# Chunks 2 to 6 of the first MLP product as seven half-size products, with one staging area for q and k and another order of work

## The chip, the cores and the metric

The kernel runs on one core of a Trainium2 chip. The metric is the device time of one execution in microseconds (us), and lower is better. The five engines of a core are named here as in the profile: PE (TensorE) multiplies, PEld is its loading of weights, DVE is VectorE, ACT is ScalarE, POOL is GpSimd, and SP issues transfers.

## What is computed

Causal attention with 16 beacon keys in front of 576 tokens, for 8 batches of 8 heads with 64 columns each, and then a two-layer MLP with a squared relu over all 4608 tokens:

```python
k_all = np.concatenate([beacon_k, k], axis=2)          # q, k, v: (8, 8, 576, 64), beacons: (8, 8, 16, 64)
v_all = np.concatenate([beacon_v, v], axis=2)
scores = scale * np.matmul(q, k_all.transpose(0, 1, 3, 2))
scores = np.where(causal, -1000000000.0, scores)       # beacons are seen by all
a = np.exp(scores - scores.max(-1, keepdims=True))
a /= a.sum(-1, keepdims=True) + 1e-09
x = np.matmul(a, v_all).transpose(0, 2, 1, 3).reshape(4608, 512)
h = x @ w_in                                           # 512 x 2048
out = (np.maximum(h, 0.0) ** 2) @ w_out                # 2048 x 512
```

## The kernel before

All work is cut into small operations with names (`add(...)` in the code). Each has the engines it may run on, what it needs, which buffers it takes from a pool and gives back, and a function that emits its instructions. A list written out in the code, `SEQUENCE`, says in which order they are emitted; `@A`, `@D` or `@P` behind a name picks ACT, DVE or POOL. Every engine then works through its own instructions strictly in that order. Nothing is decided at run time.

**Attention.** Batches 0 and 1 come in by strided transfers (`sld`, `fld`) and are transposed on PE. From batch 2 on, `ld` loads rows of q, k and v to a staging pool `stg` in fp32, `cast` writes them as bf16 to `qb`, `kb` (two areas each, used in turn) or `vb`, all on POOL, and `tr` transposes q and k by a transfer to `qT`, `kT`. Four pairs of heads make a batch. `qk` (line 631) computes transposed scores into PSUM, `exp` (L729, L653) writes exponentials to `pt` on ACT, `mask` (L750) takes the minimum with a triangle `tri` on DVE for the diagonal tiles, `av` (L771) multiplies by v with a column of ones, and `norm` (L788, L790) divides into `xn`. `xtp` with `xte` on PE, or `xt` by transfers, put the result, transposed, into the ring `xT` of 1728 tokens.

**MLP.** Nine chunks of 512 tokens. The first product of chunk j (`s1.j...`) writes to `g[j % 2]` after a relu (`relu`) and a square (`sq`); the second product (`s2.j...`) reads it, and `ev` moves its result to `osb`, which `st` stores.

- Plain form of the first product (chunks 0 to 6, L1073): 16 blocks of four matmuls of 512 columns, each block in one PSUM bank, one relu per block, one square per two blocks. Chunk 0 is done in two parts of tokens. Where the ring wraps (chunks 3 and 6) each matmul is two.
- Form with seven products (`add_first_both`, chunks 7 and 8, L950): the weights are split in four quarters, and the tokens in even and odd ones. Seven products of half size (16 matmuls of 256 columns each) replace eight. Differences of weights (`asum`, L897, kept in the q/k area when attention no longer needs it) and of inputs (`xsum`, L930) are made first. Before it, `pull` copies the ring's tokens, even and odd apart, to a dense area on POOL.
- The second product is plain in chunks 0 and 1 (L1123) and in the seven-product form from chunk 2 on (L1182); `sum` (L1154) makes its sums of `g`, in an area `sum_area` for three of them.

In the seven-product form a chain "x" uses the same PSUM bank for products 1, 6, 7 and 4: each adds to what stands there, and after each the running sum is copied out (in the first product by `hold`, named `c1`, `u2`, `u3`, and `c21` for the last; in the second by `ev`). So the next product of the chain waits for the copy. Products 5 and 3 share a chain "y" in the same way, and product 2 has a bank "z". A `plus` on DVE adds a y or z result to a held copy and writes `g`; relu and square follow as separate instructions.

PSUM has two `strip` buffers of two banks and four `ps` banks. In chunks 7 and 8 the x chain of the first product uses strips; before them the strips belong to the scores.

## Time and profile before

| | us |
|---|---|
| median of 3 runs | 329.97 (329.48 to 330.12) |
| span of the profiled execution | 327.7 |
| PE busy | 315.9 |
| DVE busy | 231.9 |
| ACT busy | 225.7 |
| POOL busy | 101.1 |

The span goes from the first to the last instruction of one profiled execution. Its own time with what lies around the instructions is not listed; the runs are 1.8 to 2.4 us longer than this span, the median 2.3. In the profile a row of a group gives the line, the engine and operation, what it writes and reads, how often it ran, its busy time, the mean time of one in ns, and the idle time before it with what ended that. A row of a timeline gives the start and the length in us first. Busy times of an engine count overlapping instructions once.

### The profile page before, as it was taken

The numbers are of one execution on the slowest core, as the hardware profiler recorded it, in microseconds if no ns is written. First come the engines' busy times: TensorE is split into PE (matmuls) and PEld (weight loads), VectorE is DVE, ScalarE is ACT, GpSimd is POOL, SyncE is SP. The second block draws the span as 40 slices with busy tenths as digits, with TensorE's granted clock in tenths as the row PEclk, the third lists the DMA queues.
The fourth block names the chain that finished last, engine by engine and source line by source line (L and its number), as shares of the span: only waits on it lengthen the run. The fifth ranks groups of instructions, "written<-read, shape, count | busy, mean of one in ns | idle before, by whom it ended". The sixth has DMA issues, their size and how long they took to land.

```text
span 327.7 us, 8732 instructions
## 1 busy us (share of the span) xinstructions
PE 315.9 (96%) x3582; PEld 227.6 (69%) x3582; DVE 231.9 (71%) x487; ACT 225.7 (69%) x332; POOL 101.1 (31%) x149
## 2 busy tenths in 40 slices
PE   2999999999999999999999999999999999999995
PEld 1478785544565558888866565776788788888884
DVE  3777886534655899587864788768865797897871
ACT  4867796458874984777766889767837664695931
POOL 9854713404532450424033403641100252000000
PEclk9999999999999999999999999999999999999999
DMA  8999998899999999999999998997913210110033
GB/s 159 220 205 215 206 169 170 168 214 204 205 177 201 240 219 171 178 244 230 180 138 215 221 181 204 202 207 156 225 23 130 46 28 2 69 61 0 2 148 111
DMA packets 145602, 51.98 MB, mean 159 GB/s; under 512 B 132506, under 2 KB 140570, under 8 KB 145562
## 3 DMA queue, kind: packets, MB, share of 16 engines
q1 hardware_dynamic: 135901, 42.32, 65.7%
q0 software_dynamic: 8512, 8.49, 15.4%
q10 hardware_dynamic: 1149, 0.62, 0.9%
q8 instruction: 28, 0.46, 0.6%
q14 instruction: 12, 0.10, 0.1%
HBM read 37.22 MB, written 9.44 MB: 142 GB/s over the span
## 4 chain that ended last, share of the span: by engine, by line
PE 85%; DMA 8%; SPq 1%; ACT 1%; POOL 1%; DVE 1%; issue 1%; ACTq 0%; POOLq 0%; DVEq 0%
PE ps L1073 26%; PE ps L1182 21%; PE ps L771 9%; PE ps L1123 8%; PE strip L631 6%; PE strip L950 4%; PE ps L950 3%; DMA stg<-in_q_dram 3%; PE strip L1182 2%; DMA kT<-qk_area 2%; PE ps L631 2%; DMA osb<-in_q_dram 2%; DMA stg<-in_v_dram 2%; PE ps L839 1%; SPq L822 1%; PE ps L474 1%
## 5 line engine op out<-in xcount | busy, mean ns | idle before, releaser
L1073 PE MATMUL ps<-xT,w_in 128*128 128x512 bf16 (+6 forms) x640 | 106.3, 315 | 0.6 <-ACT pt L729 0.6
L1073 PEld LDWEIGHTS <-w_in 128*128 128x128 bf16 x640 | 56.2, 98 | 34.8 <-issue 1.6
L729 ACT ACTIVATE pt<-strip 128x1024 bf16<-128x1024 f32 (+3 forms) x77 | 69.6, 955 | 7.8 <-PE strip L631 7.7
L1088 ACT ACTIVATE g<-ps 128x512 bf16<-128x512 f32 (+2 forms) x82 | 44.4, 551 | 20.1 <-PE ps L1073 17.2
L342 POOL CAST qk_area<-stg 128x512 bf16<-128x512 f32 (+2 forms) x60 | 39.9, 672 | 53.7 <-DMA stg<-in_k_dram 31.5
L342 POOL CAST vb<-stg 128x512 bf16<-128x512 f32 (+1 forms) x38 | 27.4, 728 | 83.6 <-DMA stg<-in_v_dram 69.4
L750 DVE TENSOR_TENSOR pt<-pt,tri 128x512 bf16<-128x512 bf16 (+1 forms) x93 | 37.8, 424 | 16.1 <-ACT pt L729 14.8
L1182 PEld LDWEIGHTS <-g 128*128 128x128 bf16 x448 | 42.9, 98 | 7.0 <-issue 0.8
L771 PEld LDWEIGHTS <-pt 128*128 128x128 bf16 x930 | 35.8, 100 | 7.0 <-issue 1.2
L771 PE MATMUL ps<-vb,pt 128*128 128x65 bf16 x930 | 38.4, 197 | 0.0
L1182 PE MATMUL ps<-w_out,g 128*128 128x256 bf16 x304 | 38.0, 273 | 0.0
L1090 DVE TENSOR_SCALAR g<-ps 128x512 bf16<-128x512 f32 (+2 forms) x46 | 27.9, 607 | 13.2 <-PE ps L1073 12.6
L1182 PEld LDWEIGHTS <-sum_area 128*128 128x128 bf16 x336 | 32.0, 98 | 5.5 <-issue 1.4
L790 DVE TENSOR_TENSOR xn<-ps,rcp 128x320 bf16<-128x320 f32 (+2 forms) x64 | 31.5, 491 | 2.2
L340 ACT COPY osb<-ps 128x512 f32<-128x512 f32 x26 | 15.2, 586 | 25.2 <-PE ps L1182 19.0
L1123 PE MATMUL ps<-w_out,g 128*128 128x512 bf16 x128 | 31.2, 379 | 0.0
L1100 DVE TENSOR_TENSOR g<-g 128x1024 bf16<-128x1024 bf16 (+2 forms) x35 | 23.4, 673 | 10.6 <-ACT g L1088 9.9
L631 PEld LDWEIGHTS <-kT 64*128 64x128 bf16 x618 | 20.0, 95 | 14.1 <-issue 10.3
L631 PE MATMUL strip<-qT,kT 64*128 64x128 bf16 (+14 forms) x500 | 29.5, 246 | 0.3 <-ACT qT L340 0.2
L1098 ACT ACTIVATE g<-g 128x1024 bf16<-128x1024 bf16 (+2 forms) x29 | 26.7, 941 | 3.0 <-DVE g L1090 2.0
L729 ACT ACTIVATE pt<-ps 128x512 bf16<-128x512 f32 x42 | 23.4, 599 | 5.7 <-PE ps L631 5.6
L1182 PE MATMUL ps<-w_sum,sum_area 128*128 128x256 bf16 x208 | 26.0, 273 | 0.0
(93 smaller groups left out, 357.7 us busy)
## 6 DMA issues: line engine op xcount, KB each, us to landing
out_dram<-osb SPq DMA_DIRECT2D x16, 512.0 KB, 3.8
stg<-in_q_dram SPq DMA_DIRECT2D x24, 256.0 KB, 4.6
stg<-in_k_dram SPq DMA_DIRECT2D x18, 256.0 KB, 5.1
stg<-in_v_dram SPq DMA_DIRECT2D x18, 256.0 KB, 4.6
w_in<-in_moe_w_in_dram POOLq DMA_DIRECT2D x4, 512.0 KB, 12.0
w_out<-in_moe_w_out_dram POOLq DMA_DIRECT2D x4, 512.0 KB, 10.9
stg<-in_v_dram POOLq DMA_DIRECT2D x6, 256.0 KB, 8.0
stg<-in_k_dram SPq DMA_DIRECT2D x6, 224.0 KB, 4.1
```

The source lines that it names most:

```text
L342: eng[e].tensor_copy(dst, src)
L631: nc.tensor.matmul(out, kT[b % 2][hp, pr, 128 * c:128 * c + 128], rhs, start=True, stop=True)
L729: nc.scalar.activation(out, in_, AF.Exp, bias=0.0, scale=scale)
L750: nc.vector.tensor_tensor(out=d, in0=d, in1=tri[0:rows, m0:m0 + m, 0:w][:, None].to_broadcast([rows, 2, m, w]), op=ALU.min)
L771: nc.tensor.matmul(a[:, at + (t - tl[0]) * (D + 1):at + (t - tl[0] + 1) * (D + 1)], P[0:rr, hj, o:o + 128], vb[b % 2][0:rr, c, 2 * pr + hj ...
L790: nc.vector.tensor_tensor(out=xn[b % 2].rearrange("p t (h d) -> p h t d", d=D)[:, h0:h0 + nh, tl[0]:tl[0] + nt], in0=a[:, :, :, 0:D], in1= ...
L1073: nc.tensor.matmul(h[:, lo - spans[0][0]:hi - spans[0][0]], w_in_sb[:, mc, ft * 128:(ft + 1) * 128], xT[:, mc, lo % RING:lo % RING + hi - lo],
L1088: nc.scalar.activation(dst, h, AF.Relu, bias=0.0, scale=1.0)
L1090: nc.vector.tensor_scalar(out=dst, in0=h, scalar1=0.0, scalar2=None, op0=ALU.max)
L1098: nc.scalar.activation(d, d, AF.Square, bias=0.0, scale=1.0)
L1123: nc.tensor.matmul(o, G[:, fc, ts * 128:(ts + 1) * 128], w_out_sb[:, fc, :], start=(fc == 0), stop=(fc == NFT - 1))
L1182: nc.tensor.matmul(o, lhs[:, f, t * 128:(t + 1) * 128], rhs[:, f], start=fresh and f == 0, stop=f == HF - 1, skip_group_check=True)
```

## The change

The first product takes the seven-product form from chunk 2 on (`BOTH = 2`). It is made in four units of two blocks of columns, each with all seven products, in `ps` banks only, and PE reads even and odd tokens straight from the ring, so that `pull` is gone. `plus` becomes one custom DVE instruction that adds and clips at zero, so that no relu follows it. q and k have one staging area instead of two, since the other holds the differences of `w_in`; a cast of batch b now needs the transposes of batch b-1. Three holding places of one bank take the place of five of two. The second product's sums 2, 3 and 4 are made in place in `g`, so that sums 2 and 4 wait for products 1 and 2. Casts may run on POOL, DVE or ACT; masks and sums on DVE or POOL, where a mask is one or two `affine_select`. The list `SEQUENCE` is another one in whole; in it 61 casts are on POOL, 20 on ACT and 19 on DVE (before: 98 on POOL, 2 on DVE), 61 masks on POOL and 35 on DVE, and 22 sums of the second product on POOL and 34 on DVE (before: all on DVE). `warm`, a tiny exponential, stands among chunk 1's operations instead of the first ones.

```diff
-    FAST, FAST_PE = 2, 0.9
-    BOTH = 7
-    NSTG, NPT, RB = 6, 3, 3
+    FAST, BOTH = 2, 2
+    NSTG, NPT, RB, NH = 6, 3, 3, 3
...
     qb = [qk_area[:, (2 * i) * W:(2 * i + 1) * W].rearrange("p (g c d) -> p g c d", g=HP, c=NT)
-          for i in range(2)]
+          for i in range(1)]
...
-    sum_area = sb("sum_area", [128, 3 * HF * HC], BF16)
+    s_sum = sb("s_sum", [128, HF, HT], BF16)
+    spare = sb("spare", [128, NH * 2 * 512 + 3 * HM * HT], BF16)
+    held = [spare[:, i * 1024:(i + 1) * 1024].bitcast(FP32) for i in range(NH)]
...
-            if b < NPE + 2:
-                deps += [zero_ops[b]]
-            else:
-                deps += trans[b - 2, x]
-        engs = ("POOL", "DVE") if b == 0 and c <= 1 else ("POOL",)
-        cast[b, x, c] = add(f"cast{b}{x}{c}", engs, {"DVE": 0.5, "POOL": 0.7}, emit_cast,
+            deps += [zero_ops[b]] if b == NPE else trans[b - 1, x]
+        cast[b, x, c] = add(f"cast{b}{x}{c}", ("POOL", "DVE", "ACT"), {"DVE": 0.5, "POOL": 0.7, "ACT": 0.58}, emit_cast,
...
+                if e == "POOL":
+                    for i in range(m):
+                        nc.gpsimd.affine_select(out=d[:, :, i], in_=d[:, :, i], compare_op=ALU.is_ge, fill=0.0,
+                                                base=Nb if m0 + i == 0 else 0, pattern=[[0, 2], [1, w]], channel_multiplier=-1)
+                    return
...
+        def in_ring(c, q):
+            return [xT[:, HM * c:HM * c + HM, lo % RING:lo % RING + hi - lo].rearrange("p m (i q) -> p m q i", q=2)[:, :, q]
+                    for lo, hi in spans]
+        b11, b12, b21, b22 = in_ring(0, 0), in_ring(0, 1), in_ring(1, 0), in_ring(1, 1)
...
+        for n, o, a, c in ((1, pieces(s[1]), b12, b11), (2, pieces(s[2]), b22, pieces(s[1])), (3, b12, b22, b12),
+                           (4, pieces(s[4]), b21, pieces(s[2]))):
...
+        def add_unit(u):
+            def product(n, chain, lhs, rhs, where, deps):
+                fresh = chain not in bank
+                def emit(e):
+                    o = ps[bank[chain].held[1]]
+                    for i in range(2):
+                        f = 2 * u + i
+                        for part, (at, w) in zip(rhs, where):
+                            for m in range(HM):
+                                nc.tensor.matmul(o[:, i * HT + at:i * HT + at + w], lhs[:, m, f * 128:(f + 1) * 128],
+                                                 part[:, m], start=fresh and i == 0 and at == 0 and m == 0, stop=m == HM - 1,
...
+            def plus(name, chain, n, dst, added, last):
+                def emit(e):
+                    nc.vector._custom_dve(TENSOR_ADD_SAT, out=dst, in0=bank_of(chain),
+                                          in1=held[keep[added].held[1]].rearrange("p (f t) -> p f t", f=2), s0=BIG, s1=0.0)
...
+            product(2, "z", A[0, 1], b21, cuts, feeds + weights)
+            product(1, "x", A[0, 0], b11, cuts, feeds + weights)
+            hold("c1", 1)
+            plus("c11", "z", 2, block(0, 0), "c1", True)
+            product(5, "y", a_sum[1], [s[1]], one, a_ops[1] + x_ops[1])
+            product(6, "x", a_sum[2], [s[2]], one, a_ops[2] + x_ops[2] + ev["c1"])
+            hold("u2", 6)
+            product(7, "x", A[1, 0], b12, cuts, a_ops[3] + x_ops[3] + ev["u2"])
+            hold("u3", 7)
+            plus("c22", "y", 5, block(1, 1), "u3", False)
+            product(4, "x", A[1, 1], [s[4]], one, x_ops[4] + ev["u3"])
+            last("c21", 4, block(1, 0))
+            product(3, "y", a_sum[4], b22, cuts, a_ops[4] + ev["c22"])
+            plus("c12", "y", 3, block(0, 1), "u2", True)
...
+            add_sum(1, s_sum, g21, g22, ALU.add, i, raw + (s2_reads[j - 1] if j > FAST else []))
+            add_sum(3, g21, g11, g21, ALU.subtract, i, sums[1][i:])
...
+            add_sum(2, g11, s_sum, g11, ALU.subtract, i, sums[3][i:] + done[1])
+            add_sum(4, g12, g12, g11, ALU.subtract, i, sums[2][i:] + done[2])
```

## Prediction

> **What bounds the kernel now.** I read four views in this order: the page, busy time by stage, TensorE's waits, and the groups by shape. From the page:

> ```profile
> span 327.7 us, 8732 instructions
> PE 315.9 (96%) x3582; PEld 227.6 (69%) x3582; DVE 231.9 (71%) x487; ACT 225.7 (69%) x332; POOL 101.1 (31%) x149
> PEclk9999999999999999999999999999999999999999
> ```

> Then busy time by stage: the start, chunks 0 and 1, the first products of chunks 2 to 6 with all that runs beside them, and the rest. Last, what TensorE waited for: total, times, longest.

> ```profile
> core 0: us, PE busy (x) PEld busy (x) DVE busy (x) ACT busy (x) POOL busy (x), PEclk, DMA share, GB/s
> 0.00:25.00 25.00, 18.23 (x218) 10.95 (x219) 15.12 (x50) 15.89 (x28) 18.82 (x34) 1.00 1.12 195
> 25.00:105.00 80.00, 79.88 (x931) 49.16 (x929) 48.06 (x111) 55.07 (x91) 30.22 (x44) 1.00 1.07 193
> 105.00:261.00 156.00, 154.87 (x1863) 111.67 (x1862) 117.76 (x243) 114.33 (x164) 44.64 (x66) 1.00 0.94 180
> 261.00:327.70 66.70, 62.91 (x577) 55.84 (x574) 50.92 (x87) 40.43 (x52) 7.42 (x6) 1.00 0.16 54
> ```

> ```profile
> PE ps L474 <- ACT qk_area L340: 5.8, 2, 5.3
> PE ps L1073 <- ACT pt L729: 0.6, 1, 0.6
> PE ps L631 <- DMA kT<-qk_area: 0.5, 1, 0.5
> ```

> TensorE is the bound. In the third stage it is busy 154.87 of 156 us at full clock, and in the whole run its waits after the start are 0.6 and 0.5 us. VectorE is at 75% there and ScalarE at 73%. So time goes down only where TensorE gets less to do, and only as long as the other two keep its cover. The span is 327.7 us; the median of the runs, 329.97, is 2.3 above it, and I add that 2.3 to every sum.

> **TensorE's part.** A busy matmul may be a waiting one, so I price them from runs without a break in the chain that ended last.

> ```profile
> 68.46 9.50 PE ps L1073 x44
> 160.95 4.37 PE ps L1182 x40
> ```

> Forty-four matmuls of 512 columns take 9.50 us (216 ns each), forty of 256 columns 4.37 us (109 ns). A plain first product is 64 of the first kind, 13.82 us; seven half-size products of 16 each are 112 of the second, 12.23 us. That is 1.59 us less per chunk and **-7.9 us** for chunks 2 to 6. Chunks 3 and 6 wrap in the ring, which cuts four of their seven products in two; their plain products are cut in the same place today, so I count nothing, within 0.3.

> **What ScalarE, VectorE and GpSimd get.** Rows for the prices:

> ```profile
> L340 ACT COPY osb<-ps 128x512 f32<-128x512 f32 x26 | 15.2, 586 | 25.2 <-PE ps L1182 19.0 <-PE ps L1123 5.3 <-DMA out_dram<-osb 0.8
> L1088 ACT ACTIVATE g<-ps 128x512 bf16<-128x512 f32 x64 | 37.8, 599 | 16.9 <-PE ps L1073 14.5 <-DVE rcp L788 1.9
> L1098 ACT ACTIVATE g<-g 128x1024 bf16<-128x1024 bf16 x21 | 21.9, 1055 | 2.9 <-DVE g L1090 2.0 <-DVE pt L750 0.4 <-DVE rcp L788 0.2
> L997 DVE TENSOR_TENSOR g<-ps,stg 128x512 bf16<-128x512 f32 x16 | 10.7, 684 | 3.4 <-PE ps L950 3.4
> L1100 DVE TENSOR_TENSOR g<-g 128x1024 bf16<-128x1024 bf16 x27 | 20.2, 749 | 10.1 <-ACT g L1088 9.5
> L750 DVE TENSOR_TENSOR pt<-pt,tri 128x512 bf16<-128x512 bf16 x62 | 29.5, 478 | 11.8 <-ACT pt L729 10.5 <-ACT pt L653 1.1
> L750 DVE TENSOR_TENSOR pt<-pt,tri 80x160 bf16<-80x160 bf16 x31 | 9.7, 315 | 4.3 <-ACT pt L729 4.3
> L1154 DVE TENSOR_TENSOR g<-g 128x1024 bf16<-128x1024 bf16 x14 | 10.3, 740 | 0.0
> L342 POOL CAST qk_area<-stg 128x512 bf16<-128x512 f32 x48 | 32.5, 680 | 43.8 <-DMA stg<-in_k_dram 24.6 <-DMA stg<-in_q_dram 18.8
> L342 POOL COPY pt<-xT 128x512 bf16<-128x512 bf16 x4 | 5.9, 1508 | 3.8 <-DMA xT<-xn 3.8
> L327 POOL TENSOR_SCALAR_AFFINE_SELECT tri<-tri 128x128 bf16<-128x128 bf16 x4 | 1.0, 296 | 0.1
> ```

> I counted both orders from chunk 2's first `s1` to chunk 7's. ScalarE loses 50 relus (-30.0 us at 599) and gains 48 `hold` and `c21` evacuations (+28.3 at 586 to 599), 13 squares (+13.7 at 1055), 10 casts (+5.9 at the copy's 586) and about 2 us of exponentials that fall into the stage: **+20, to 134 us**. VectorE gains 60 additions into `g` (+41.2 at 684 to 688), 32 evacuations (+22), 14 differences `xsum` (+9.6) and 9 casts (+3.8); it loses 30 relus (-20.7), 13 squares (-9.8 at 749), 32 long and 12 short masks (-19.1 at 478 and 315), 9 sums (-6.6 at 740) and the three `asum` (-3.7): about **+17.4, to 135.2 us**. That the added relu rides in the custom addition for nothing is a bound from below; `xsum` has no row in its new strided form, so between 0.41 and 0.75 I take 0.69. GpSimd gives away 17 casts and 4 pulls and gets the 44 masks, 9 sums and 6 differences. A mask there is two selects of 256 columns, between 0.30 and 0.59 each by the 296 ns row, taken at 0.38. A sum has two inputs of 1024 columns, between 1.4 (twice 680) and 3.0 (twice 1508), taken at 2.1. GpSimd comes to about **84 us** from 44.6. TensorE has 154.9 - 7.9 = 147 us of work in the stage, so both helpers go from about 75% to 92% of it. They still fit, but little is left over.

> **The x chain.** A unit keeps products 1, 6, 7, 4 in one PSUM bank, and each must be copied out before the next adds to it. What such a link needs is in the timeline, at `ev3.u2`:

> ```profile
> 165.80 1.92 PE L1182 MATMUL ps<-w_sum,sum_area 128*128 128x256 bf16 x16
> 166.88 0.59 ACT L340 COPY osb<-ps 128x512 f32<-128x512 f32 x1 [0.17 <-PE ps L1182]
> 167.55 1.04 PE L1182 MATMUL ps<-w_out,g 128*128 128x256 bf16 x8
> ```

> The product's eight matmuls end at 165.80 + 8 x 0.109 = 166.67; the copy starts 0.21 later, takes 0.59, and the next product starts 0.08 after it: 0.88 us, or 0.98 with VectorE's 0.69. The new order has 112 links (16 a chunk: three in x, one in y). I added up the TensorE work it puts between the ends of each. In 28 links that is less than the need, most by 0.01 to 0.11 (0.87 of cover, two half products), and in chunk 7's first unit 0.44 and 0.00. The shortfalls sum to **+3.3 us**, 1.8 in chunks 2 to 6 and 1.6 in chunk 7. Bounds: zero if the work in front runs late anyway, 6 if 65 links with under 1.35 of cover each lose 0.05 more behind a busy engine.

> **The start.**

> ```profile
> 2.36 1.28 ACT L554 ACT_TABLE_LOAD   x1 [2.36 <-issue]
> 10.60 0.41 DVE L750 TENSOR_TENSOR sum_area<-sum_area,tri 128x512 bf16<-128x512 bf16 x1
> 10.78 3.08 POOL L863 DMA_DIRECT2D w_in<-in_moe_w_in_dram  x4
> 15.83 0.84 PE L771 MATMUL ps<-vb,pt 128*128 128x65 bf16 x12
> ```

> `warm`, which brings the table load to an idle ScalarE at 2.36, moves to chunk 1. The load then comes before the first exponential, with the scores of other pairs queued behind it: 0 to 1.28, taken at 0.6. Masks 3 and 0 and the casts of v0 and v1 go to GpSimd behind all its loads, which end at 13.86 today; two masks and two casts put the first `av` near 16.7 instead of 15.83. The scores now ahead of it hide half: 0.4. `tri` loses two selects of 0.30 in front, a gain of up to 0.6. Together -0.6 to +2.2, taken as **+1.0**.

> **Edits at nothing.** One staging area: casts of batch b wait for the transposes of b-1, and between a batch's last cast and its first scores the order has 3 to 9 us of TensorE work, where today's order has 8 to 11. SP's queue holds the `xt` transposes and `ld` v behind each `tr`; v is needed later still. Without this cover the 0.5 us wait in the list above grows. `zero` and the smaller `tri` come once. Chunks 7 and 8 lose pulls and separate relus beside a TensorE that was full anyway.

> **Sum.** I leave 0.8 for VectorE being late (0 to 10.4, next part). 327.7 - 7.9 + 3.3 + 1.0 + 0.8 = 324.9, and with the 2.3: **327.2 us**.

> **Rival 1, slower: VectorE becomes the bound through GpSimd.**

> ```profile
> 113.97 0.41 DVE L750 TENSOR_TENSOR pt<-pt,tri 128x512 bf16<-128x512 bf16 x1
> 115.62 0.62 POOL L342 CAST qk_area<-stg 128x512 bf16<-128x512 f32 x1 [0.59 <-DMA stg<-in_q_dram]
> 115.66 0.85 DVE L750 TENSOR_TENSOR pt<-pt,tri 128x512 bf16<-128x512 bf16 x1
> ```

> The same mask takes 0.41 with GpSimd idle and 0.85 when a cast runs on GpSimd: it waited for it. In the new stage 73 VectorE instructions (masks, squares, sums, differences, casts) can meet this; today 119, but with half the GpSimd time against them. VectorE has 147 - 135.2 = 11.8 us to give away. If every second of the 73 waits for a mean GpSimd instruction (84 us over 137, 0.61), that is 22 us and the stage takes 135.2 + 22 = 157.4 instead of 156; with the start and chunk 7's links (1.0 and 1.6) the run takes 330 + 1.4 + 2.6 = **334 us**. From every fourth on it decides. Against it: fewer instructions are exposed, and the additions, with one input in PSUM, are not. [...]

> **Rival 2, slower: TensorE reads the ring more slowly.** Four of the seven products now read every second column of `xT`, in chunks 7 and 8 too, where pulls made them dense.

> ```profile
> 11.65 0.53 PE L631 MATMUL strip<-qT,kT 64*128 64x240 bf16 x4
> 15.37 0.53 PE L631 MATMUL strip<-qT,kT 64*128 64x336 bf16 x4
> ```

> The only spread reads today are batch 0's scores: 736 columns (240 and 128 twice) 120 apart take the 0.53 us of 832 dense ones (336 and 80 twice), 13% more. On 64 matmuls of 109 ns in 7 chunks that is +6.4: **333.6 us**. For nothing speaks that a step of two is far nearer to dense than 120. [...]

> **Rival 3, no change:** links and VectorE together eat the 7.9: **330**. **Rival 4, all of it arrives:** no link costs anything and the start gains: 327.7 - 7.9 - 0.6 + 2.3 = **321.5**.

> **Chances.** Forecast 0.48, rival 1 0.31, rival 2 0.08, rival 3 0.08, rival 4 0.05. Under 0.2% (0.66 us) a measurement of this kernel can't tell from no change. Faster is forecast and rival 4, 0.53; same 0.08; slower 0.39. The likeliest case alone reaches from 322.5 to 329. The range goes from 321.5 (rival 4) to 336 (rival 1 with 55 of 100 exposed instructions waiting instead of 50).

> **What would show it.** Right: 320 matmuls of 512 columns fewer and 560 of 256 more, but for the cuts; TensorE near 308 us busy; short waits of `s1` products on `hold` copies, together 2 to 5 us; the table load directly before the first exponential. VectorE 140 to 147 us busy in the middle stage. Wrong: matmuls of 256 columns over 120 ns (rival 2); VectorE over 150 us there, with sums and masks well above 0.74 and 0.48 (rival 1); or TensorE waiting for scores on `kT` transposes.

## The result and the profile after

The changed kernel takes **346.4 us** (345.4 to 346.7), the kernel before on the same chip 329.7. The ratio is 1.050, with a 95% interval of 1.046 to 1.054. The prediction of 327.2 (321.5 to 336) was wrong in sign and in range. The profiled execution took 346.7 us with a span of 345.0. Ratios below are against the kernel before on the same chip, with 95% intervals. Times are medians of all runs, while the ratios leave out seven runs in a slower state, so the two can differ by a little. The experiments ran on several chips, on which the kernel before took 328.7 to 329.7 us; differences in us are taken from 346.4 and are good to about 1 us, and where two intervals overlap, the text says so.

The page of the changed kernel, with the shares of the chain that ended last:

```profile
span 345.0 us, 9430 instructions
PE 315.6 (91%) x3822; PEld 245.7 (71%) x3822; DVE 249.6 (72%) x495; ACT 234.6 (68%) x356; POOL 160.3 (46%) x237
PEclk9999999999999999999899999999999999999998
PE 61%; DMA 16%; DVE 12%; ACT 3%; issue 3%; POOL 2%; SPq 1%; DVEq 0%; ACTq 0%; POOLq 0%
```

TensorE has 3822 matmuls, the 240 more that were to be expected, but it is busy just as long as before (315.6 to 315.9), and the span is 17.3 us longer. Its share of the chain is 61%; before it was 85%. Busy time by stage (start; chunks 0 and 1; first products of chunks 2 to 6; the rest):

```profile
core 0: us, PE busy (x) PEld busy (x) DVE busy (x) ACT busy (x) POOL busy (x), PEclk, DMA share, GB/s
0.00:25.00 25.00, 16.81 (x208) 11.41 (x210) 13.80 (x39) 14.28 (x24) 18.00 (x35) 1.00 1.11 198
25.00:102.00 77.00, 75.17 (x888) 47.09 (x885) 54.24 (x124) 53.48 (x89) 27.33 (x48) 1.00 0.98 187
102.00:279.00 177.00, 163.83 (x2205) 136.28 (x2203) 141.89 (x270) 134.39 (x191) 90.45 (x143) 0.99 0.86 162
279.00:345.00 66.00, 59.84 (x528) 50.94 (x528) 39.72 (x64) 32.42 (x52) 24.51 (x11) 0.99 0.18 59
```

The whole loss lies in the third stage: chunk 2's first product starts at 105.0 (105.2 before), chunk 7's at 279.8 (263.5 before), and from there to the end it is 65.2 us against 64.2. The stage is longer and TensorE is less full: 163.8 of 177, beside VectorE at 80%, ScalarE at 76% and the transfers at 0.86 instead of 0.94. Nothing is saturated, so something is late. TensorE's waits name it:

```profile
PE strip L638 <- DMA kT<-qk_area: 8.4, 4, 3.3
PE ps L446 <- DVE w_sum L439: 3.5, 1, 3.5
PE strip L638 <- DVE kT L353: 2.3, 1, 2.3
PE ps L967 <- DMA xT<-xn: 1.7, 2, 1.0
PE ps L967 <- ACT spare L351: 1.4, 2, 0.7
PE ps L1176 <- DVE g L1145: 1.3, 1, 1.3
PE ps L967 <- DVE g L1005: 1.3, 2, 1.0
...
PE ps L638 <- DMA kT<-qk_area: 0.7, 1, 0.7
```

The second and third rows lie in the start. Of the others the transposes of k are far ahead: 9.1 us in five waits, where before 0.5 us stood. (One of the five, 1.8 us for batch 2, lies before chunk 2's first product, in a stretch that lost no time as a whole.) This is the longest of them, batch 5: GpSimd's last casts, SP's queue, TensorE.

```profile
158.31 1.17 POOL L353 CAST qk_area<-stg 128x512 bf16<-128x512 f32 x2
155.37 4.40 SPq L425 DMA_TRANSPOSE qT<-qk_area  x1
159.82 1.09 SPq L1107 DMA_DIRECT2D out_dram<-osb  x2
161.01 4.92 SPq L425 DMA_TRANSPOSE kT<-qk_area  x1
164.98 1.08 PE L783 MATMUL ps<-vb,pt 128*128 128x65 bf16 x30
169.38 1.03 PE L638 MATMUL strip<-qT,kT 64*128 64x240 bf16 x10 [3.31 <-DMA kT<-qk_area]
```

The casts end at 159.48. A store stands in front of the transpose on SP. It is issued at 161.01, takes 4.92 us on the queue, and lands at 169.3, so the chain needs 9.9 us. TensorE has work until 166.06, that is 6.6 us of cover. The same place before:

```profile
152.66 1.36 POOL L342 CAST qk_area<-stg 128x512 bf16<-128x512 f32 x2 [0.18 <-DMA stg<-in_k_dram]
155.66 3.90 SPq L418 DMA_TRANSPOSE kT<-qk_area  x1
165.25 0.61 PE L631 MATMUL strip<-qT,kT 64*128 64x240 bf16 x10
```

There the chain needs 7.6 us (casts end at 154.02, the transpose lands at 161.6) and has 11.2. Over batches 2 to 7 the chain needs 6.7 to 9.9 us in the changed kernel and has a cover of 5.5 to 7.4; before, it needed 5.0 to 8.3 and had 6.5 to 11.2. So the need grew a little, and in five of the six batches the cover shrank below it.

**Where 16.9 us went.** A stalled matmul counts as busy (the 256-column ones last 272 to 276 ns in the mean, but follow each other 109 to 114 ns apart), so I added up from start to start. 320 matmuls of 512 columns at 216 ns have gone and 560 of 256 at 109 ns have come, 7.9 us less than before (the 20480 columns alone are worth the 8.5 that some expectations below speak of); reads of every second column cost 2.0 more (below); and gaps of over 60 ns between matmuls grew from 10.3 to 33.0 us, +22.7. In these gaps 1.0 us of slower matmuls at a granted clock of 0.50 after one wait is counted (last section). That is +16.8 against the measured 345.0 - 25.4 - (327.7 - 25.0) = 16.9, chunk 1's first block starting at 25.4 and 25.0. So the saved matmuls are all there, and nearly three times as much has come as waiting.

### The profile page after: what moved, and what is told of

It reads as the page before. It is cut to its first block, busy times and chain, and to the rows that moved or that the text cites. A ratio compares the mean times of both kernels' runs of the same rounds, so it can differ in the third digit from the quotient of the medians.

```text
span 345.0 us, 9430 instructions
## 1 busy us (share of the span) xinstructions
PE 315.6 (91%) x3822; PEld 245.7 (71%) x3822; DVE 249.6 (72%) x495; ACT 234.6 (68%) x356; POOL 160.3 (46%) x237
## 4 chain that ended last, share of the span: by engine, by line
PE 61%; DMA 16%; DVE 12%; ACT 3%; issue 3%; POOL 2%; SPq 1%; DVEq 0%; ACTq 0%; POOLq 0%
PE ps L1176 18%; PE ps L967 18%; PE ps L1070 6%; DMA kT<-qk_area 6%; PE ps L1119 5%; PE ps L783 5%; PE strip L638 4%; DMA stg<-in_k_dram 3%; DVE g L1005 3%; DMA stg<-in_q_dram 3%; DMA stg<-in_v_dram 2%; PE strip L1176 2%; DVE xn L802 2%; PE ps L638 1%; DVE pt L763 1%
## 5 line engine op out<-in xcount | busy, mean ns | idle before, releaser
L1005 DVE CUSTOM_DVE_ANT_0 g<-ps,spare 128x512 bf16<-128x512 f32 x84 | 56.9, 686 | 19.0 <-PE ps L967 16.4
L759 POOL TENSOR_SCALAR_AFFINE_SELECT pt<-pt 128x256 bf16<-128x256 bf16 (+1 forms) x101 | 39.3, 417 | 62.2 <-ACT pt L736 57.7
L967 PEld LDWEIGHTS <-w_in 128*128 128x128 bf16 x544 | 44.6, 96 | 12.4 <-issue 2.3
L967 PE MATMUL ps<-xT,w_in 128*128 128x256 bf16 (+4 forms) x432 | 49.2, 250 | 3.5 <-DMA xT<-xn 1.7
L1031 ACT ACTIVATE g<-g 128x1024 bf16<-128x1024 bf16 x44 | 45.4, 1059 | 4.7 <-DVE g L1005 4.4
L351 ACT COPY spare<-ps 128x512 f32<-128x512 f32 x57 | 33.4, 590 | 20.3 <-PE ps L967 19.8
L1145 POOL TENSOR_TENSOR g<-g 128x1024 bf16<-128x1024 bf16 x14 | 30.3, 2174 | 28.2 <-PE ps L1176 10.7
L967 PEld LDWEIGHTS <-qk_area 128*128 128x128 bf16 x368 | 32.4, 97 | 9.5 <-issue 3.7
L638 PE MATMUL strip<-qT,kT 64*128 64x208 bf16 (+16 forms) x500 | 29.3, 249 | 10.7 <-DMA kT<-qk_area 8.4
L967 PE MATMUL ps<-spare,qk_area 128*128 128x256 bf16 x224 | 33.0, 272 | 0.8 <-DVE spare L943 0.5
L1070 PE MATMUL ps<-xT,w_in 128*128 128x240 bf16 (+2 forms) x192 | 30.6, 309 | 0.0
L351 ACT COPY osb<-ps 128x512 f32<-128x512 f32 x23 | 13.5, 587 | 20.0 <-PE ps L1176 18.7
```

Of the source, the lines that this page charges most:

```text
L351: nc.scalar.copy(dst, src)
L638: nc.tensor.matmul(out, kT[b % 2][hp, pr, 128 * c:128 * c + 128], rhs, start=True, stop=True)
L759: nc.gpsimd.affine_select(out=d[:, :, i], in_=d[:, :, i], compare_op=ALU.is_ge, fill=0.0, base=Nb if m0 + i == 0 else 0, pattern=[[0, 2], ...
L967: nc.tensor.matmul(o[:, i * HT + at:i * HT + at + w], lhs[:, m, f * 128:(f + 1) * 128], part[:, m], start=fresh and i == 0 and at == 0 and ...
L1005: nc.vector._custom_dve(TENSOR_ADD_SAT, out=dst, in0=bank_of(chain), in1=held[keep[added].held[1]].rearrange("p (f t) -> p f t", f=2), s0= ...
L1031: nc.scalar.activation(both, both, AF.Square, bias=0.0, scale=1.0)
```

## The experiments

The first question was which lateness costs the time: late scores (theory), VectorE late behind GpSimd (rival), spread reads, the links of the x chain, SP's queue, or the one staging area. Each has one kernel that takes it away, as far as possible alone.

**Scores that wait for no transpose.** From batch 2 on the scores read columns of `w_in` in place of `qT` and `kT`, and as much is multiplied.

```diff
-            nc.tensor.matmul(out, kT[b % 2][hp, pr, 128 * c:128 * c + 128], rhs, start=True, stop=True)
+            lhs = kT[b % 2][hp, pr, 128 * c:128 * c + 128]
+            if b >= NPE:
+                lhs, rhs = w_in_sb[hp, pr, 128 * c:128 * c + 128], w_in_sb[hp, pr, 384 + t0:384 + t1]
+            nc.tensor.matmul(out, lhs, rhs, start=True, stop=True)
```

> From the third batch on the scores read columns of the input weights in place of `kT` and `qT`, so the transposed queries and keys are made but not used; all else is as in the changed kernel. Theory 1 (late transposes): the 16.5 us were lost mostly where TensorE waited for `kT`; the waits of 8.4 and 0.7 us in the list of waits, 10.0 us with the restart behind each, go away, and nothing else is late in their place: 336 to 338 us. Rival 2 (late helpers): VectorE, ScalarE and GpSimd are behind TensorE anyway and catch up while it waits for `kT`; without these waits the same time turns up as waits for ACT, DVE and POOL: 342 us or more. Rival 3 (the single staging area): the casts wait for the transposes of the batch before; they still do, so the loads and casts stand where they stood, but nobody waits for them: 336 to 338 us too; the next kernel but two tells this one apart.

340.55 us, ratio 1.034 (1.030 to 1.037): 5.9 us less, the largest effect of a single cause, but of the 9.1 us of waits only two thirds come back. These are now the largest after the start:

```profile
PE ps L970 <- DVE g L1008: 3.1, 3, 1.8
PE ps L970 <- DMA xT<-xn: 1.9, 2, 1.0
```

In the changed kernel TensorE waited 1.3 us for the additions into `g` and 1.7 for `xT`. So more of the additions' lateness shows once the scores are in time.

**GpSimd without masks and sums.** Its masks from batch 2 on and its sums aren't computed.

```diff
-                    for i in range(m):
+                    for i in range(m if b < 2 else 0):
...
-... lambda e: (nc.vector if e == "DVE" else nc.gpsimd).tensor_tensor(out=o[:, fs], in0=a[:, fs], in1=c[:, fs], op=op)
+... lambda e: nc.vector.tensor_tensor(out=o[:, fs], in0=a[:, fs], in1=c[:, fs], op=op) if e == "DVE" else None
```

> GpSimd's masks from the third batch on and its 22 sums of the second product are left out (the probabilities above the diagonal stay, the sums are not made); its casts, its first-product sums and all that the other engines do stay. [...] Theory 1 (late transposes): casts move up a little behind the missing masks, the transposes with them by about a third, and the 2 to 3 us of waits on sums and masks go: 339 to 343 us. [...]

343.8 us, 1.044 (1.040 to 1.049): 2.6 less, with intervals that overlap, and the waits for `kT` are the same 8.4. With both edits together:

> The two edits of e1_aside (scores read the input weights, nobody waits for the transposes) and e2_noport (GpSimd's masks and second-product sums left out) together. Measured apart they gave 5.85 and 2.6 us. If the late transposes and the helpers are two losses one after the other, the sum: 338 us. If the helpers are late because of GpSimd and only the waits for `kT` hid this in e2_noport (VectorE caught up in them), more than the sum comes back: 334 us or less. If what is left has its cause neither in the transposes nor in GpSimd's masks and sums, but in the order in which ScalarE's and VectorE's links stand, 337 us or more.

338.59 us, 1.028 (1.025 to 1.031). 7.8 us less, of 8.5 if they were independent: the two gains add up, and they leave half of the 16.7.

**Even and odd tokens as two dense halves.** The first half of a chunk takes the place of the even tokens, so the rows of the output come in another order.

```diff
-rearrange("p m (i q) -> p m q i", q=2)[:, :, q]
+rearrange("p m (q i) -> p m q i", q=2)[:, :, q]
```

> In chunks 2 to 8 a block of the first product takes neighbouring columns of `xT` (first and second half of each span) in place of every second one; the order is the same, the output's rows come in another order. TensorE: 448 matmuls (7 chunks, 4 units, 4 of the 7 products, 4 each) at 109 in place of 114 ns, 2.0 us less. VectorE: the 18 sums of columns of `xT` at 0.41 in place of 0.69 us, 5 us less. Theory 1 (late transposes): the columns are not what is late; the 2 us show where TensorE does not wait for `kT` afterwards: 344 to 346.5 us. Rival 2 (late helpers): VectorE comes 5 us earlier and TensorE with it: 338 to 341 us.

344.3 us, 1.046 (1.040 to 1.053), 2.1 less; the intervals overlap, so the matmuls themselves have to show it. The first product's matmuls that read `xT`, the differences `xsum`, and a group that reads a dense area, in the changed kernel:

```profile
L967 PE MATMUL ps<-xT,w_in 128*128 128x256 bf16 x240 | 35.1, 275 | 1.7 <-DMA xT<-xn 1.0 <-ACT spare L351 0.7
L967 PE MATMUL ps<-spare,qk_area 128*128 128x256 bf16 x224 | 33.0, 272 | 0.8 <-DVE spare L943 0.5
L943 DVE TENSOR_TENSOR spare<-xT,spare 128x512 bf16<-128x512 bf16 x9 | 6.5, 720 | 0.2
```

The mean says little (275 to 272, from start to end); from start to start they are 114 ns apart against 109, on 448 matmuls 2.0 us. With dense columns these too are 109 ns apart, and the `xsum` row falls from 720 to 453.

**One staging area in the kernel before.** Its order as it is, `qb` and `kb` with one area, casts of batch b after the transposes of b-1.

```diff
-                in_=srcb[b % 2].rearrange("p g c d -> p (g c d)"),
+                in_=srcb[0].rearrange("p g c d -> p (g c d)"),
...
-            if b < NPE + 2:
-                deps += [zero_ops[b]]
-            else:
-                deps += trans[b - 2, x]
+            deps += [zero_ops[b]] if b == NPE else trans[b - 1, x]
```

> The kernel before with one staging area for the casts in place of two, and nothing else changed: a batch's casts wait until the transposes of the batch before have read the area. Theory 1 (the new order is late, not the area): in the kernel before a batch's casts start 13 to 22 us after the transposes of the batch before have landed, so nothing waits: 329 to 331 us. Rival 3 (the single staging area is the loss): the casts are held back and the transposes come late here too: 335 us or more.

329.61 us, 1.001 (0.997 to 1.004). The area costs nothing in that order. In the new order it was not tried alone, but the changed kernel's trace shows no wait for it: from batch 3 on a batch's first cast starts 11.7 to 15.0 us after k of the batch before has landed. So what makes k late is the short way from cast to scores, not the lack of a place.

**Shorter links.** `hold`, `last` and `plus` work on 256 of the 512 columns in chunks 2 to 8; the other half isn't written.

```diff
-                    copy_on(e, held[box["op"].held[1]], ps[bank["x"].held[1]])
+                    copy_on(e, held[box["op"].held[1]][:, 0:HT], ps[bank["x"].held[1]][:, 0:HT])
...
-                        nc.scalar.activation(dst, bank_of("x"), AF.Relu, bias=0.0, scale=1.0)
+                        nc.scalar.activation(dst[:, 0], bank_of("x")[:, 0], AF.Relu, bias=0.0, scale=1.0)
...
```

> In the first products of chunks 2 to 8 every copy, clip and add behind a product (196 of them) handles the first 256 of its 512 columns only; the other half of the hidden values stays what it was. Products, order and everything else are the changed kernel's. By the shorter forms of the traces (0.37 in place of 0.58 us on ScalarE, 0.42 in place of 0.69 us on VectorE) this takes 16 us off ScalarE and 31 us off VectorE. Theory 2 in its sharper form (the links behind the products, and what they hold up on VectorE and ScalarE, are the second half of the loss): the waits for these links, some 8 us, go, and casts and sums come earlier with them: 334 us or less. Theory 1 alone (late transposes by the written order): the 10 us for `kT` stay and 3 to 5 us of the others go: 340 to 343 us.

341.27 us, 1.040 (1.032 to 1.048): 5.1 less, with intervals that just overlap. The waits for `kT` stay, 8.6. This also takes 20 us of work from VectorE and 7.6 from ScalarE in the middle stage (121.95 and 126.84), so the 5.1 holds the links and this work together.

**Less on SP's queue.** The 30 loads of v from batch 2 on are not issued; the casts of v read what is there.

```diff
+            if x == "v" and b >= 2:
+                return [None]
```

> The 30 loads of values of batches 2 to 7 are not issued; their casts still run, on whatever lies in the staging slot. Rival 4 (SyncE's queue): in the stretch from chunk 2 to chunk 7 this queue issues for 121 us of 177 and stands waiting for 49 us, loads and stores in it hold up the transposes behind them. Without a third of its loads (0.8 us each, 24 us in all, and the waits for a free staging slot in front of them) the transposes of `kT` and `xT` come earlier: 341 us or less. If the queue only mirrors casts and norms that are late themselves: 344 us or more.

349.74 us, 1.060 (1.053 to 1.066). The share of the transfers in the middle stage falls to 0.64, the waits for `kT` are 8.0, and the kernel is not faster (3.3 us slower, with intervals that overlap). So the transfers as a whole are not the bound in this order.

**Three at once:** scores aside, GpSimd without masks and sums, shorter links.

> The three edits that each gave something in the changed kernel's own order, together: scores do not wait for the transposes (5.85 us alone), GpSimd's masks and second-product sums are left out (2.6 us alone), the work behind the first product's halves is halved (5.1 us alone). If these are three losses that stand side by side, the sum: 333 us, still slower than the kernel before, and 3 us and more of the loss would have yet another cause. If each hid the others (TensorE in front of one late thing lets the others catch up), more than the sum: 327 to 331 us; then TensorE's 8.5 us less work shows at last.

337.37 us, 1.028 (1.022 to 1.034). 9.0 less, where the three singly make 13.5. Scores aside and GpSimd without masks and sums stood at the same ratio, 1.028, without the shorter links, so here these add nothing that can be measured. What is late now:

```profile
PE ps L970 <- DMA xT<-xn: 4.4, 4, 1.9
PE ps L970 <- DVE g L1008: 2.0, 3, 1.2
```

**Five at once:** these three, dense columns, and no loads of v.

> The three edits of e13_three (scores read the input weights, GpSimd's masks and second-product sums left out, the work behind the first product's halves halved) together with the two of e4_dense (neighbouring columns) and e10_sp (30 loads of values not issued), all in the changed kernel's own order. In e13_three 5 us of waits for `xT` were the largest left. If these come from SyncE's queue, and the rest is TensorE's slower reads: 2 us for the columns and some 4 us for `xT`: 329 to 332 us. If the order itself lets norms and features come late, the waits stay and only the columns give: 334 to 337 us. The seven products can be called worth their 8 us only below 328 us.

328.76 us (326.0 to 331.0), 0.998 (0.995 to 1.001). The two added edits, which alone gave -2.1 and +3.3, now give -8.6, which fits that the transfers of `xT` had come to be what is late; which of the two did it these runs don't tell apart. The chain is TensorE's again at 83%, and the largest wait after the start is for VectorE:

```profile
PE ps L972 <- DVE spare L948: 2.9, 2, 2.1
```

Its gaps sum to 18.9 us, of which 2.3 are eleven matmuls that this trace has no record of; that is some 6 us above the kernel before, and it eats most of the 7.9 that TensorE saves. Even without five of its burdens the new form is not faster.

The second question was whether the loss lies in this order of the operations or in the form. The next five kernels keep all the work and change only the list of words (names of operations). A word without a letter runs on the first engine that it may run on.

**Only loads, casts and transposes of q and k moved.** Batch 5, as an example:

```diff
-... s1.3.0.4 ... tr5q ... s1.3.2.7 ... s1.3.3.2 ... cast5k4@P ... tr5k ...
+... s1.3.0.4 ... tr5q ... s1.3.2.7 cast5k4 ... s1.3.3.2 ... tr5k ...
```

> The changed kernel with its work and its engine letters as they are; in the written order only the loads and casts of queries and keys of batches 2 to 7 and the 12 transposes are moved, earlier in most batches (the first load of batches 4, 5 and 7 by 35, 26 and 11 TensorE words). The order had been made with 3.7 us for a transpose on its queue and 3.8 us to its landing; the trace shows 3.1 to 5.2 us and 5.0 to 8.8 us. Theory 1 (late transposes, through the order alone): the waits for `kT` go from 10 us to under 4 us, and of these 6 us the kernel keeps as much as e1_aside kept, 60%: 341 to 344 us, and not under 340.5 us, where e1_aside stood with no such wait at all. If moving the casts relieves the helpers as well, under 340.5 us.

348.81 us, 1.054 (1.048 to 1.061), so none of the gain came. The waits of `strip` for `kT` fell from 8.4 to 2.6, as was meant, and masks and casts on the helpers became late:

```profile
PE ps L777 <- POOL pt L753: 3.1, 4, 1.9
PE strip L632 <- DMA kT<-qk_area: 2.6, 1, 2.6
PE ps L777 <- DVE vb L347: 1.7, 1, 1.7
```

**Only the helpers' words moved** (copies, masks, casts of v, sums). By the two lists 150 of them go to another engine, not the 74 that the expectation speaks of.

```diff
-cast2v4@P ... cast5v0@P ... ev1.2@A ... h2.0.u2@A
+cast2v4@A ... cast5v0@D ... ev1.2@D ... h2.0.u2@D
```

> The changed kernel with the order of TensorE, of SyncE and of the loads and casts of queries and keys as it is; only the words of ScalarE, VectorE and GpSimd between them (evacuations, adds, sums, masks, squares, norms, exponentials, casts of values) are moved and 74 of them change engine. It tells whether the rest of the loss is the placement of the helpers' work or its amount. Placement: the waits for ACT and DVE beside the 10 us for `kT` are some 13 us longer than before; most of them go, and some of `kT` with them: 332 to 338 us. Amount (VectorE 142 us and ScalarE 134 us of a stage of 177 us, with links that cannot be met): 342 us or more.

345.73 us, 1.048 (1.045 to 1.051): no change.

**Every word from batch 2's loads on may move.** The list was made with durations from the changed kernel's trace, VectorE's waits for GpSimd among them.

```diff
-... s2.1.2.3 ... qk12.5 ... s1.3.3.2 ... cast5k4@P ... tr5k ...
+... s2.1.0.3 ... qk12.5 ... s2.2.3.0 ... cast5k4 ... s2.2.3.1 ... tr5k ...
```

> [...] If both losses are the order and not the seven products, TensorE is left with its work, 8.5 us less than before and 2 us more for every second column, and with waits of a few us: 323 to 328 us, faster than the kernel before (329.2 us). If the seven products in the middle need more of ScalarE and VectorE than lies beside TensorE's work, no order helps: 332 us or more.

347.47 us, 1.052 (1.046 to 1.059). No wait for a transpose of k is left, and the gaps sum to 33.8 us, as much as in the changed kernel (33.0). The places have changed:

```profile
PE ps L1170 <- ACT osb L345: 3.9, 2, 2.2
...
PE ps L961 <- DVE g L999: 2.2, 4, 1.1
PE ps L632 <- DVE g L1080: 2.0, 1, 2.0
```

Two more lists, made with other prices for the helpers:

> The changed kernel's instructions in another written order from the loads of batch 2 on, made as for e8_order but counting what the traces since showed: VectorE's casts from staging wait for GpSimd as its sums do, loads take 0.8 us of SyncE's queue, and three sets of scattered durations at once, so that no link stands without slack. Loads of batches 4, 5 and 7 stand earlier, squares have moved from ScalarE to VectorE. If the loss is one of order: 325 to 333 us. If ScalarE, VectorE and GpSimd cannot carry the seven products beside the attention at TensorE's pace: 338 us or more, whatever the order.

> The changed kernel's instructions, tiles and sizes unchanged, only the written order and the engine letters from the loads of batch 2 on made as for e14_dense3. It is the same kernel form as e8_order and e11_order2, which took 347.5 and 348.7 us. [...]

348.67 us, 1.058 (1.055 to 1.062), and 345.23 us, 1.048 (1.043 to 1.053). The first shows rival 1's wait of VectorE for GpSimd at its longest:

```profile
187.73 3.05 POOL L753 TENSOR_SCALAR_AFFINE_SELECT pt<-pt 80x160 bf16<-80x160 bf16 x8
190.75 4.19 POOL L1139 TENSOR_TENSOR g<-g 128x1024 bf16<-128x1024 bf16 x2
188.74 6.47 DVE L757 TENSOR_TENSOR pt<-pt,tri 128x512 bf16<-128x512 bf16 x1
195.14 0.68 DVE L999 CUSTOM_DVE_ANT_0 g<-ps,spare 128x512 bf16<-128x512 f32 x1
```

A mask, 0.48 us in the mean before, took 6.47 us beside ten instructions of GpSimd, which followed each other without a break and ended at 194.94, 0.27 before the mask. The addition behind it kept TensorE waiting 5.6 us.

The last question was whether any version is better. **Dense halves, with stores that put the rows back in place, and an order of its own**; nothing is left out.

```diff
-rearrange("p m (i q) -> p m q i", q=2)[:, :, q]
+rearrange("p m (q i) -> p m q i", q=2)[:, :, q]
...
+                for lo, hi in spans_of(t0, t1):
+                    at, w = (lo - t0) // 2, (hi - lo) // 2
+                    if w == TCH // 2:
+                        insts.append(nc.sync.dma_start(
+                            out=out[lo + v * w:lo + v * w + w, :].rearrange("(t p) d -> p t d", t=2), in_=osb[v]))
...
```

> As e11_order2, with an order of its own, and the blocks of chunks 2 to 8 made of neighbouring columns of `xT` (first and second half of each span, with the output's rows stored to match, three transfers in place of one in the two chunks that wrap around). TensorE 2 us less, VectorE's sums of columns 0.41 in place of 0.69 us: 323 to 331 us if the loss is one of order; 2 to 4 us under e11_order2 in any case.

336.04 us, 1.019 (1.016 to 1.022): 10.4 better than the change, 6.3 worse than before. Its largest wait after the start is one of 2.6 us for a sum. Three more orders of the same kernel, the first made to allow for waits as long as that mask's:

> [...] If the seven products leave ScalarE, VectorE and GpSimd too little room in any order: 332 us or more.

> [...] e12_dense2 took 336.0 and e14_dense3 338.9 us. If the orders failed on what they did not count: 327 to 332 us. If each order only exchanges one late thing for another: 334 to 340 us.

> A second order made in the same way as e17_dense4, from e12_dense2's, to see how far two such orders differ: within 3 us of e17_dense4 if what was counted is what decides, more if the order decides by chance.

338.90 us, 1.030 (1.024 to 1.036); 336.72 us, 1.024 (1.018 to 1.030); and 337.62 us, 1.018 (1.009 to 1.026), with single runs of this last one from 332.6 to 344.9. So the orders that count more waits are no better than the first one. What goes with the better times is the dense halves with their stores: the four lists of this kernel take 336 to 339 us, the six lists without them, the change's own among them, 345 to 349. For two lists made in the same way, on the same chip, it is 338.90 against 345.23, three times the 2.1 of the single edit; how much of that is VectorE's shorter `xsum` or the stores was not separated. No version beat the kernel before.

## Why the prediction was wrong

**The step that failed is "Edits at nothing".** It gave 3 to 9 us of TensorE work between a batch's last cast and its first scores, said that this cover can go, and counted nothing. What the chain needs was never set against it, though before's rows had it: casts end at 154.02, k lands at 161.6, 7.6 us, already more than most of "3 to 9". It needs 6.7 to 9.9 in the changed kernel. The prediction names this wait among its signs of being wrong, but gives it no term, no rival and no chance. The price, by taking the wait away: 5.9 us of the 19.2 that the forecast missed. The staging area, with which that step began, is innocent (1.001, and no wait for it in the changed trace).

**Terms that were mis-sized.** The x chain was counted at 3.3; its edit gives up to 5.1 alone, less work on the helpers included, and nothing that can be measured on top of the first two edits. VectorE's lateness behind GpSimd was counted at 0.8, with 10.4 at most; leaving out GpSimd's masks and sums gives 2.6. Spread reads were set at 0 in the sum and 6.4 in rival 2; they cost 2.0 on TensorE itself, and dense halves are worth some 6 between two lists made in the same way. There the row of batch 0's scores pointed the right way at a third of the size: with a step of two a matmul took 114 ns instead of 109. The start was counted at +1.0; chunk 1 begins 0.4 us later, and by chunk 2 nothing is left of it (105.0 against 105.2). The table load stands where it stood, at 2.36 and 1.28 us long.

**What was right.** TensorE's part: -7.9 forecast, and the two prices behind it, 216 and 109 ns, stand in the changed trace too. The helpers' loads in the middle stage, measured over 102 to 279: ScalarE 134 forecast and 134.4 found; VectorE 140 to 147 with the waits for GpSimd, and 141.9 found (the changes listed for it add up to +16.7, not +17.4); GpSimd 84 and 90.5, largely as its 84 selects took 428 ns instead of 380. These prices were read well from a trace that had none of these operations:

```profile
L1005 DVE CUSTOM_DVE_ANT_0 g<-ps,spare 128x512 bf16<-128x512 f32 x84 | 56.9, 686 | 19.0 <-PE ps L967 16.4 <-ACT spare L351 1.4 <-DVE spare L353 0.2
L759 POOL TENSOR_SCALAR_AFFINE_SELECT pt<-pt 128x256 bf16<-128x256 bf16 x84 | 33.8, 428 | 38.7 <-ACT pt L736 36.3 <-PE ps L967 1.9 <-DMA stg<-in_q_dram 0.5
L1145 POOL TENSOR_TENSOR g<-g 128x1024 bf16<-128x1024 bf16 x14 | 30.3, 2174 | 28.2 <-PE ps L1176 10.7 <-DVE g L1145 10.6 <-PE ps L967 6.5
```

The clipped addition does carry its relu for nothing (686 ns against 684).

**The method failed too.** The sum adds delays of single steps to TensorE's work and takes the rest for hidden. With these terms put right, in the order they were named, it comes to 327.2 + 5.9 + 1.8 + 1.8 + 2.0 - 1.0 = 337.7 at most. The other 8.7 us no single edit shows: one edit at a time gives 5.9, 5.1, 2.6, 2.1 and -3.3, together 12.4; all five at once give 17.6. Some of the waits only come to light when others are gone: additions behind scores, `xT` behind both.

**Rival 1** named a wait that is there, with the wrong role. Beside GpSimd a mask took up to 1.01 us in the middle stage (0.41 at the shortest), a cast 0.83 (0.42), a sum 1.63 (0.68), a difference 2.17 (0.68) and a square 2.28 (0.68), while the 84 additions, one input of which is in PSUM, took 674 to 693 ns each, 51 of them with a GpSimd instruction running. VectorE is busy 80% of the middle stage, so it isn't the bound. Its 334 would have needed 22 us of lost VectorE time. Measured against the shortest of each form, the VectorE instructions that use only SBUF lost some 7 us in the middle stage, and the edit shows 2.6 us of the run's time.

**What stays open.** Whether an order exists in which the new form beats 329.7: ten lists lie between 336 and 349, but they are no proof. Which of five-at-once's last two edits freed `xT` wasn't separated, and shorter links were not run with the scores aside alone. That all units share four `ps` banks was not varied either.

## What to carry to other kernels

Before work is taken from an engine that is 99% busy, write down for each chain of transfers what it needs from its last input to its landing, and what cover the new order leaves: a cover that shrinks from 11.2 to 6.6 us against a need of 7.6 (9.9 in the end) is a cost that no busy time shows. A new wait hides the waits behind it, so undo the suspects one at a time and then together; if the single gains and the joint gain differ, several chains may be about equally late, and moving operations can then only change which of them is last, as the five lists here did.

## What the runs showed of the hardware that was not expected

**The clock can fall after a wait.** Behind the longest wait for k, in busy time by stretch (the third number from the end is TensorE's granted clock), with the product that follows:

```profile
165.50:169.00 3.50, 0.57 (x19) 0.44 (x15) 3.36 (x10) 1.77 (x2) 2.12 (x1) 1.00 1.19 146
169.10:172.50 3.40, 3.12 (x21) 2.02 (x22) 0.84 (x2) 1.94 (x2) 0.00 (x0) 0.50 1.01 193
172.50:176.00 3.50, 3.50 (x34) 3.14 (x33) 2.15 (x4) 0.59 (x1) 0.76 (x1) 1.00 0.62 132
```

**VectorE's wait can last over many GpSimd instructions, but does not always.** The 6.47 us mask above ended only after ten. In the changed kernel a sum on VectorE ended while the second ran:

```profile
211.50 1.50 POOL L943 TENSOR_TENSOR spare<-xT,spare 128x512 bf16<-128x512 bf16 x1 [5.15 <-DMA stg<-in_v_dram]
211.93 2.92 DVE L1145 TENSOR_TENSOR g<-s_sum,g 128x1024 bf16<-128x1024 bf16 x2
212.96 0.77 POOL L759 TENSOR_SCALAR_AFFINE_SELECT pt<-pt 80x160 bf16<-80x160 bf16 x1
```

The first of the two sums, 0.68 us long alone, ended at 213.55, 0.55 after GpSimd's addition, while GpSimd's next instruction was already there and took 0.77 instead of its mean of 0.36. What decides is not shown.

**Spread reads** of every second bf16 column cost TensorE 4 to 5%, 114 ns against 109.
